# An attention-then-expert-layer kernel: the first chain rebuilt, v block 0 turned on TensorE, the sums of w_out moved later, the last products reordered and their stores spread over three engines

## The chip, the cores and the metric

The kernel runs on one core of one Trainium2 chip. The metric is device time in microseconds (us) of one execution, read as the median of several. A program on one core has no second die to compare with, so a run counts as fast unless it lies over 1.5% above the fastest of its kernel.

## The reference

```python
def attn(q, k, v, tau):                        # q, k, v: 4 x 6080 x 256
    qn = q / (norm(q, axis=1) + 1e-06); kn = k / (norm(k, axis=1) + 1e-06)
    s = kn.transpose(0, 2, 1) @ qn / tau       # 256 x 256 per batch
    a = softmax(s, -1)
    return v @ a
def moe(x, w_in, w_out):                       # x: 24320 x 256
    h = x @ w_in                               # 256 x 2048
    return gelu_tanh(h) @ w_out                # 2048 x 256
```

The score matrix of a batch needs all rows of q and k of that batch. Only then can a product with v start. That is why the first batch has a long start in which DMA is the busy one: in the first three of the 40 slices of the kernel before, DMA is busy at 9 tenths and PE at 3, 7 and 7.

## The kernel before

Per batch the kernel folds the softmax into W_in (`AW = softmax * W_in`, 256 x 2048), so that a block of 512 rows of v needs two stages: `AW` times v (called `mm1`, output tile `hp`, followed by Gelu into tile `g`), and Gelu's output times w_out (`mm2`). The second stage uses seven products on half-size blocks instead of eight, and for this needs seven combinations of quarters of w_out, `wcomb`. There are 48 blocks, 12 to a batch. q and k of the next batch are loaded, squared and multiplied while the blocks of the present one run.

First, w_out as loaded lies in a buffer of the pool that also holds `g`; that pool has two buffers, so `g` of block 1 takes the buffer that w_out leaves. Its load is issued by SP, behind the transpose of v block 1:

```python
    def load_wout():
        w = gp.tile([128, FC, 256], FP32, tag="g", name="wst")
        WST.append(w)
        nc.sync.dma_start(out=w, in_=moe_w_out.rearrange("(t p) d -> p t d", p=128))
    # ... the order of the program:
        cast_v(1)        # GpSimd: v to bf16 in DRAM
        load_vt(1)       # SP: transpose of what the cast wrote
        load_wout()      # SP
```

Second, two of the combinations are plain casts on GpSimd and five are made on DVE (called its sums below). They stand among the eight steps `p` of block 0, ahead of the loads of q and k of batch 1, which GpSimd issues too:

```python
    def prep_wout(step):
        if step == 0:
            nc.gpsimd.tensor_copy(wc(A11), w_half(0, 0))
            nc.gpsimd.tensor_copy(wc(A12), w_half(0, 1))
            # ... DVE sums of steps 0, 1 and 2 left out
    # ... in the loop over blocks n and steps p:
                if n == 0 and p in (2, 4, 5):
                    prep_wout((2, 4, 5).index(p))
                # ...
                    if p in (2, 5) and blk < ncn:
                        load_one(nxt, blk, p // 5, gate)   # q at p == 2, k at p == 5
```

Third, the last block has its second stage alone, in the order of all others, and one store of four DMAs from SP:

```python
        for bi in range(4):
            nc.sync.dma_start(out=dst[bi], in_=ot[bi * 32 : bi * 32 + 32, ...])
```

## Time and profile before

| | before |
|---|---|
| median | 735.85 us (3 runs, 735.68 to 735.98) |
| profiled span | 735.3 us |
| PE busy | 700.1 us (95%) |
| first product with v | 47.09 us |
| last first-stage product | 721.60 us |
| from there to the end of the span | 13.7 us |

The last three rows cut the run into a start, a middle and a tail. PE is busy almost without a gap in the middle, so a change can win or lose only at the two ends. The lines of the profile are in the prediction below. Two more are from the timeline of the kernel before (start, us, engine, line, operation, tiles; in square brackets the idle time before it and what ended it): when GpSimd issues the first load of batch 1, and when the first Gelu of block 1 starts.

```profile
58.96 0.56 POOL L89 DMA_DIRECT2D t<-in_q_dram  x1
64.22 1.02 ACT L325 ACTIVATE g<-hp 128x1024 bf16<-128x1024 f32 x1 [0.73 <-PE hp L321]
```

The load is issued only after w_out has landed (55.42), and the Gelu waits for nothing but PE.

### The profile page before, as it was taken

The page shows a single profiled execution, that of the slowest core. Times are in us where ns is not written, and L with a number is a line of the kernel's source. Part 1 is how long each engine was busy: PE and PEld are TensorE (multiplying, and loading weights), DVE is VectorE, ACT ScalarE, POOL GpSimd, SP SyncE. Part 2 cuts the span into 40 slices and gives each one's busy share as a digit, 9 for nine tenths or more (in the row PEclk, how much of TensorE's full clock was granted, in tenths as well). Part 3 has the DMA queues.
Part 4 walks back from the last instruction along what each step waited for, and adds up shares of the span by engine and source line. Part 5 has one row for each costly group of instructions (what it writes and reads, how often), then busy time and mean ns, then how long its engine had stood idle before and what let it go on. Part 6 is the DMA issues. An engine that isn't in the chain of part 4 may idle for free.

```text
span 735.3 us, 11988 instructions
## 1 busy us (share of the span) xinstructions
PE 700.1 (95%) x4760; PEld 466.6 (63%) x4760; DVE 500.5 (68%) x882; ACT 483.6 (66%) x592; POOL 72.2 (10%) x133
## 2 busy tenths in 40 slices
PE   3777999999999999999999999999999999999996
PEld 2434666666666666666666666666666666666664
DVE  1339787877766787787685777787686465564654
ACT  3365677677667766776666677677666767676672
POOL 4303111110001110110100111111000000000000
PEclk9998999999999999999999999999999999999999
DMA  9995797885437868884455888688334636455233
GB/s 175 203 229 98 123 142 113 129 129 90 67 58 128 135 115 130 133 138 76 77 86 80 130 136 138 108 138 133 56 58 69 100 58 99 74 92 80 47 53 55
DMA packets 164841, 78.65 MB, mean 107 GB/s; under 512 B 152497, under 2 KB 156337, under 8 KB 164017
## 3 DMA queue, kind: packets, MB, share of 16 engines
q0 software_dynamic: 12192, 38.41, 34.0%
q1 hardware_dynamic: 152592, 39.47, 31.7%
q8 instruction: 37, 0.61, 0.3%
q14 instruction: 20, 0.16, 0.1%
HBM read 78.91 MB, written 37.36 MB: 158 GB/s over the span
## 4 chain that ended last, share of the span: by engine, by line
PE 86%; DMA 6%; DVE 4%; issue 1%; ACT 1%; POOL 0%; SPq 0%; DVEq 0%; POOLq 0%
PE hp L321 42%; PE r L414 22%; PE p L414 11%; PE q L414 5%; PE G L175 5%; DMA t<-in_q_dram 2%; DMA t<-in_k_dram 1%; PE ps L297 1%; DMA wst<-in_moe_w_out_dram 1%; DVE dn L274 1%; DMA vb<-in_v_dram 1%; DVE c L430 1%; DVE aw L304 1%; DVE t L385 0%; ACT th L266 0%
## 5 line engine op out<-in xcount | busy, mean ns | idle before, releaser
L325 ACT ACTIVATE g<-hp 128x1024 bf16<-128x1024 f32 (+1 forms) x384 | 387.9, 1015 | 205.3 <-PE hp L321 202.4
L321 PE MATMUL hp<-vT,aw 128*128 128x512 bf16 (+1 forms) x1536 | 389.9, 379 | 4.7 <-DVE aw L304 4.7
L414 PEld LDWEIGHTS <-wcomb 128*128 128x128 bf16 x2688 | 262.7, 98 | 104.7 <-issue 8.8
L321 PEld LDWEIGHTS <-aw 128*128 128x128 bf16 x1536 | 150.3, 98 | 115.2 <-DVE aw L304 5.2
L414 PE MATMUL r<-t,wcomb 128*128 128x256 bf16 (+1 forms) x1152 | 148.0, 271 | 5.2 <-DVE c L430 5.2
L175 PE MATMUL G<-t 128*128 128x256 bf16 (+1 forms) x384 | 69.9, 284 | 16.3 <-DMA t<-in_k_dram 16.3
L430 DVE TENSOR_TENSOR c<-r,y 128x256 f32<-128x256 f32 (+1 forms) x96 | 40.3, 420 | 52.5 <-PE r L414 48.0
L430 DVE TENSOR_TENSOR c<-q,x 128x256 f32<-128x256 f32 (+1 forms) x48 | 20.2, 420 | 73.1 <-PE q L414 71.3
L398 DVE TENSOR_TENSOR t<-t,g 128x1024 bf16<-128x1024 bf16 (+1 forms) x96 | 65.0, 677 | 0.0
L397 DVE TENSOR_TENSOR t<-g 128x1024 bf16<-128x1024 bf16 (+1 forms) x96 | 64.9, 676 | 0.0
L396 DVE TENSOR_TENSOR t<-g,t 128x1024 bf16<-128x1024 bf16 (+1 forms) x96 | 63.4, 661 | 0.1
L137 ACT ACTIVATE sq<-t 128x1536 bf16<-128x1536 bf16 (+4 forms) x31 | 46.2, 1491 | 23.0 <-PE ss L188 12.0
L107 POOL DMA_DIRECT2D vb<-in_v_dram x48 | 24.1, 503 | 365.7 <-PE hp L321 365.2
L438 DVE STREAM_TRANSPOSE ot<-c 128x256 f32<-128x256 f32 (+1 forms) x144 | 57.5, 425 | 2.0 <-DVE c L430 0.4
L385 DVE TENSOR_TENSOR t<-g 128x2048 bf16<-128x2048 bf16 (+1 forms) x48 | 57.7, 1203 | 0.0
L175 PEld LDWEIGHTS <-t 128*128 128x128 bf16 (+1 forms) x384 | 38.7, 102 | 29.7 <-issue 12.0
L414 PE MATMUL r<-g,wcomb 128*128 128x256 bf16 (+1 forms) x384 | 49.4, 272 | 0.0
L414 PE MATMUL p<-t,wcomb 128*128 128x256 bf16 (+1 forms) x384 | 49.3, 271 | 0.0
L414 PE MATMUL q<-g,wcomb 128*128 128x256 bf16 (+1 forms) x384 | 49.3, 271 | 0.0
L414 PE MATMUL p<-g,wcomb 128*128 128x256 bf16 (+1 forms) x384 | 49.3, 271 | 0.0
L138 DVE TENSOR_TENSOR sq<-t 128x1536 bf16<-128x1536 bf16 (+4 forms) x31 | 29.8, 962 | 26.4 <-DMA t<-in_k_dram 26.0
L438 DVE STREAM_TRANSPOSE ot<-r 128x256 f32<-128x256 f32 (+1 forms) x48 | 21.4, 445 | 31.0 <-PE r L414 31.0
(74 smaller groups left out, 293.8 us busy)
## 6 DMA issues: line engine op xcount, KB each, us to landing
out_dram<-ot SPq DMA_DIRECT2D x176, 128.0 KB, 2.9
vb<-in_v_dram POOLq DMA_DIRECT2D x44, 256.0 KB, 5.1
t<-in_q_dram POOLq DMA_DIRECT2D x21, 384.0 KB, 4.9
t<-in_k_dram POOLq DMA_DIRECT2D x21, 384.0 KB, 4.4
t<-in_q_dram POOLq DMA_DIRECT2D x5, 512.0 KB, 13.0
t<-in_k_dram POOLq DMA_DIRECT2D x5, 512.0 KB, 14.9
wst<-in_moe_w_out_dram SPq DMA_DIRECT2D x1, 2048.0 KB, 10.9
out_dram<-ot SPq DMA_DIRECT2D x16, 112.0 KB, 2.7
```

Source lines behind the costliest of these rows:

```text
L137: nc.scalar.activation(sq[:, 0:n, 0:256], qt[:, 0:n, :], AF.Square)
L138: nc.vector.tensor_mul(sq[:, 0:n, 256:512], kt[:, 0:n, :], kt[:, 0:n, :])
L175: nc.tensor.matmul(G[b][:, jc, :], lhsT=qt[:np_, r, jc * 128 : jc * 128 + 128], rhs=kt[:np_, r, :], start=first and jc == 0, stop=last and ...
L321: mm = nc.tensor.matmul(hp[:, u, :cols], lhsT=AW[b][:, cc, fc * 128 : fc * 128 + 128], rhs=vt_tiles[n][:, cc, :cols], start=cc == 0, stop= ...
L325: nc.scalar.activation(GS[n][:, 2 * p : 2 * p + 2, :cols], hp[:, :, :cols], AF.Gelu_apprx_tanh)
L385: nc.vector.tensor_sub(t1[:, :, :hc], quarter(n, 0, 1), quarter(n, 0, 0))
L396: nc.vector.tensor_sub(v[2], b22, v[1])
L397: nc.vector.tensor_sub(v[3], b22, quarter(n, 0, 1, f0, f1))
L398: nc.vector.tensor_sub(v[4], v[2], quarter(n, 1, 0, f0, f1))
L414: nc.tensor.matmul(ACCS[n, acc][:, :hc], lhsT=wcomb[:, w, fc, :], rhs=x, start=first and fc == 0, stop=fc == 7, skip_group_check=True)
L430: nc.vector.tensor_add(CS[n][:, tj, ci, :hc], ACCS[n, acc][:, :hc], XS[n, name][:, :hc])
L438: nc.vector.transpose(OT[n][:, tj * nb : tj * nb + nb, ci, :], src.rearrange("p (x t) -> p x t", t=32))
```

## The change

The intent is to start block 0 sooner and to end the last block sooner. The last chunk of q and k is smaller, and the rows left over go with the first; the norms of q come out of one-column products; v block 0 is no longer cast and transposed by DMA but loaded behind k and turned on TensorE, and fourteen products that nobody uses (`warm`) stand ahead of the score matrix; W_in's first part goes ahead of v; the sums of w_out move to steps 6 and 7 of block 0; and the last block's products have an order in which no two in a row use one accumulator, with its stores cut in halves and spread over three engines. The core of the diff:

```diff
-        sizes = [8, 8, 8, 8, 8, 4, 3] if b == 0 else [6, 6, 6, 6, 6, 6, 6, 5]
+        sizes = [7, 8, 8, 8, 8, 6, 2] if b == 0 else [6, 6, 6, 6, 6, 6, 6, 5]
 ...
-        cast_v(0)
-        load_vt(0)
 ...
         for fs in range(4):
             nc.gpsimd.dma_start(out=win_bf[...], in_=wi[...])
+            if fs == 0:
+                nc.gpsimd.dma_start(out=v0, in_=v[0, 0:BLK, :].rearrange("(s p) c -> p s c", p=128))
         cast_v(1)
         load_vt(1)
         load_wout()
         cast_v(2)
+        warm(14)
         scores(0)
-        row_sums(0)
-        aw_part(0, 0, 0, "dve", "r")
-        aw_part(0, 0, 1, "act", "q")
+        first_vt()
+        first_aw()
 ...
-                if n == 0 and p in (2, 4, 5):
-                    prep_wout((2, 4, 5).index(p))
+                if n == 0 and p in (6, 7):
+                    prep_wout(p - 6)
 ...
+    def mm2_last(n):
+        # ... products 1, 5, 6, 2, 7, 3 with their adds and transposes
+        store_half(n, 1, (nc.sync, nc.gpsimd, nc.sync, nc.gpsimd))
+        product(n, 4, "r", False)
+        turn(n, 1, 0, ACCS[n, "r"][:, :hc])
+        store_half(n, 0, (nc.scalar, nc.sync, nc.scalar, nc.sync))
```

More of the change, by code (lines that the diff above doesn't have):

```diff
@@ L74, in chunks_of, with with_rest @@
         return res
+    def with_rest(b, c):
+        return REM > 0 and c == (0 if b == 0 else len(chunks_of(b)) - 1)
     qk_tiles = {}
@@ L85, in load_one @@
         r0, n = chunks_of(b)[c]
-        last = r0 + n == R
         t = qkp.tile([128, 8, 256], BF16, tag="qk"[which])
@@ L91, in load_one @@
             in_=src[b, 0 : R * 128, :].rearrange("(p r) c -> p r c", r=R)[:, r0 : r0 + n, :]), gate)
-        if last and REM:
+        if with_rest(b, c):
             after(nc.gpsimd.dma_start(out=t[:REM, n, :], in_=src[b, R * 128 : N, :]), gate)
@@ L118, in load_vt @@
         vt_tiles[n] = vT
-    G, SS, ACC, SQ = {}, {}, {}, {}
+    G, SS, ACC, SQ, SQR = {}, {}, {}, {}, {}
     def rows_of(b, c):
@@ L125, in rows_of @@
         rows = [(r, 128) for r in range(n)]
-        if r0 + n == R and REM:
+        if with_rest(b, c):
             rows.append((n, REM))
@@ L132, in squares @@
         r0, n = chunks_of(b)[c]
-        last = r0 + n == R
+        rest = with_rest(b, c)
         sq = sqp.tile([128, 8, 512], BF16, tag="sq")
-        if last and REM:
+        if rest:
             nc.vector.memset(sq[REM:, n, :], 0.0)
-        nc.scalar.activation(sq[:, 0:n, 0:256], qt[:, 0:n, :], AF.Square)
+        if n <= 2:
+            nc.vector.tensor_mul(sq[:, 0:n, 0:256], qt[:, 0:n, :], qt[:, 0:n, :])
+        else:
+            nc.scalar.activation(sq[:, 0:n, 0:256], qt[:, 0:n, :], AF.Square)
         nc.vector.tensor_mul(sq[:, 0:n, 256:512], kt[:, 0:n, :], kt[:, 0:n, :])
-        if last and REM:
+        if rest:
             nc.scalar.activation(sq[:REM, n, 0:256], qt[:REM, n, :], AF.Square)
@@ L142, in squares, with fold_rows @@
         SQ[b, c] = sq
+    def fold_rows(b, c):
+        n = len(rows_of(b, c))
+        if n == 8:
+            a1 = addp.tile([128, 4, 512], BF16, tag="a1")
+            nc.vector.tensor_add(a1, SQ[b, c][:, 0:4, :], SQ[b, c][:, 4:8, :])
+            SQ[b, c] = a1
+            n = 4
+        SQR[b, c] = n
     def sum_rows(b, c):
@@ L179, in gram_row, with ss_rows @@
                 start=first and jc == 0, stop=last and jc == 1)
-    def ss_row(b, c, i):
-        if (b, c, i) == (b, 0, 0):
-            SS[b] = pM.tile([128, 512], FP32, tag="q", name=f"ss{b}")
-        rows = rows_of(b, c)
-        r, np_ = rows[i]
-        first = c == 0 and i == 0
-        last = c == len(chunks_of(b)) - 1 and i == len(rows) - 1
-        nc.tensor.matmul(SS[b], lhsT=ones_bf[:np_, :], rhs=SQ[b, c][:np_, r, :],
-                         start=first, stop=last)
-    def ss_acc(b):
-        nc.tensor.matmul(SS[b], lhsT=ones_f, rhs=ACC[b], start=False, stop=False)
+    def ss_rows(c, which):
+        last = c == len(chunks_of(0)) - 1
+        if c == 0:
+            SS[which] = pM.tile([128, 2] if which == 0 else [128, 256], FP32,
+                                tag="qp"[which], name=f"ss0{which}")
+        sq = SQ[0, c]
+        n = SQR[0, c]
+        for r in range(n):
+            if which == 0:
+                for jc in range(2):
+                    nc.tensor.matmul(SS[0][:, jc : jc + 1],
+                                     lhsT=sq[:, r, jc * 128 : jc * 128 + 128],
+                                     rhs=ones_bf[:, 0:1],
+                                     start=c == 0 and r == 0 and jc == 0,
+                                     stop=last and r == n - 1 and jc == 1)
+            else:
+                nc.tensor.matmul(SS[1], lhsT=ones_bf, rhs=sq[:, r, 256:512],
+                                 start=c == 0 and r == 0, stop=last and r == n - 1)
     def ss_cols(b):
@@ L201, with q_factor @@
     ET, RS = {}, {}
+    def q_factor():
+        lnq = smx.tile([128, 2], FP32, tag="lnq")
+        nc.scalar.activation(lnq, SS[0], AF.Ln, bias=eps)
+        rq = smx.tile([128, 2], FP32, tag="rq")
+        nc.scalar.activation(rq, lnq, AF.Exp, scale=-0.5, bias=log_it)
+        RQ.append(rq)
+    RQ = []
     def scores(b):
-        ss = SS[b]
         lnk = smx.tile([128, 256], FP32, tag="lnk")
-        nc.scalar.activation(lnk, ss[:, 256:512], AF.Ln, bias=eps)
-        qq = smx.tile([128, 2], FP32, tag="qq")
-        for jc in range(2):
-            junk = smx.tile([128, 128], FP32, tag="junk")
-            nc.vector.scalar_tensor_tensor(
-                junk, ss[:, jc * 128 : jc * 128 + 128], 1.0, ident,
-                op0=ALU.mult, op1=ALU.mult, accum_out=qq[:, jc : jc + 1])
+        nc.scalar.activation(lnk, SS[1], AF.Ln, bias=eps)
         rk = smx.tile([128, 256], FP32, tag="rk")
         nc.scalar.activation(rk, lnk, AF.Exp, scale=-0.5)
-        lnq = smx.tile([128, 2], FP32, tag="lnq")
-        nc.scalar.activation(lnq, qq, AF.Ln, bias=eps)
-        rq = smx.tile([128, 2], FP32, tag="rq")
-        nc.scalar.activation(rq, lnq, AF.Exp, scale=-0.5, bias=log_it)
         S = smx.tile([128, 2, 256], FP32, tag="S")
@@ L224, in scores, with first_vt, first_aw, warm @@
         for jc in range(2):
-            nc.scalar.activation(eT[:, jc, :], S[:, jc, :], AF.Exp, scale=rq[:, jc : jc + 1])
+            nc.scalar.activation(eT[:, jc, :], S[:, jc, :], AF.Exp, scale=RQ[0][:, jc : jc + 1])
         ET[b] = eT
+    def first_vt():
+        ps = pM.tile([128, 2, BLK], BF16, tag="r", name="vt_ps")
+        for s in range(BLK // 128):
+            for cc in range(2):
+                nc.tensor.transpose(ps[:, cc, s * 128 : s * 128 + 128],
+                                    v0[:, s, cc * 128 : cc * 128 + 128], ident_bf)
+        vT = vts.tile([128, 2, BLK], BF16, tag="vT", name="vT_first")
+        nc.vector.tensor_copy(vT[:, 0, :], ps[:, 0, :])
+        nc.scalar.activation(vT[:, 1, :], ps[:, 1, :], AF.Copy)
+        vt_tiles[0] = vT
+    def first_aw():
+        b = 0
+        AW[b] = awp.tile([128, 2, D], BF16, tag="aw", name=f"aw{b}")
+        ps = [pM.tile([128, 512], FP32, tag="qp"[ic], name=f"aw_ps{ic}") for ic in range(2)]
+        sums = pM.tile([128, 2], FP32, tag="a", name="sums0")
+        rs = smx.tile([128, 2], FP32, tag="rs")
+        e = lambda jc, ic: ET[b][:, jc, ic * 128 : ic * 128 + 128]
+        for jc in range(2):
+            for ic in range(2):
+                nc.tensor.matmul(ps[ic], lhsT=e(jc, ic), rhs=win_bf[:, jc, 0:512],
+                                 start=jc == 0, stop=jc == 1)
+        for ic in range(2):
+            for jc in range(2):
+                nc.tensor.matmul(sums[:, ic : ic + 1], lhsT=e(jc, ic), rhs=ones_bf[:, 0:1],
+                                 start=jc == 0, stop=jc == 1)
+        nc.vector.reciprocal(rs, sums)
+        RS[b] = rs
+        for f in range(2):
+            for ic in range(2):
+                nc.vector.tensor_scalar_mul(AW[b][:, ic, f * 256 : f * 256 + 256],
+                                            ps[ic][:, f * 256 : f * 256 + 256], rs[:, ic : ic + 1])
+    def warm(n):
+        w = pH.tile([128, 2, 512], FP32, tag="h", name="warm")
+        for i in range(n):
+            nc.tensor.matmul(w[:, 0, 0:256], lhsT=ones_bf, rhs=zeros_bf, start=True, stop=True)
     NRM, TH = {}, {}
@@ L279, in row_sums @@
     def row_sums(b):
-        ps = pM.tile([128, 2], FP32, tag="p" if b == 0 else "q")
+        ps = pM.tile([128, 2], FP32, tag="q")
         for ic in range(2):
@@ L360, in prep_wout @@
         if step == 0:
+            t = sqp.tile([128, 2, 32, 32], FP32, tag="sq", name="wf")
+            WF.append(t)
             nc.gpsimd.tensor_copy(wc(A11), w_half(0, 0))
             nc.gpsimd.tensor_copy(wc(A12), w_half(0, 1))
-            t = sqp.tile([128, 2, 32, 32], FP32, tag="sq", name="wf")
-            WF.append(t)
             nc.vector.tensor_add(t[:, 0], w_half(1, 0), w_half(1, 1))
             nc.vector.tensor_copy(wc(S1), t[:, 0])
+            nc.vector.tensor_sub(t[:, 1], t[:, 0], w_half(0, 0))
         if step == 1:
             t = WF[0]
-            nc.vector.tensor_sub(t[:, 1], t[:, 0], w_half(0, 0))
             nc.vector.tensor_copy(wc(S2), t[:, 1])
             nc.vector.tensor_sub(wc(S4), w_half(0, 1), t[:, 1])
-        if step == 2:
             nc.vector.tensor_sub(wc(S3), w_half(0, 0), w_half(1, 0))
@@ L470, in mm2, with store_half @@
             turn(n, 1, 0, ACCS[n, "r"][:, :hc])
+    def mm2_last(n):
+        hc = cols_of(n) // 2
+        product(n, 1, "r", True)
+        keep(n, "r", "x1")
+        product(n, 5, "p", True)
+        keep(n, "p", "y5")
+        sums_2(n, 4, 8)
+        product(n, 6, "r", False)
+        keep(n, "r", "y53")
+        product(n, 2, "q", True)
+        add_out(n, "q", "x1", 0, 0)
+        turn(n, 0, 0, CS[n][:, 0, 0, :hc])
+        product(n, 7, "r", False)
+        add_out(n, "r", "y5", 1, 1)
+        turn(n, 1, 1, CS[n][:, 1, 1, :hc])
+        product(n, 3, "p", False)
+        add_out(n, "p", "y53", 0, 1)
+        turn(n, 0, 1, CS[n][:, 1, 0, :hc])
+        store_half(n, 1, (nc.sync, nc.gpsimd, nc.sync, nc.gpsimd))
+        product(n, 4, "r", False)
+        turn(n, 1, 0, ACCS[n, "r"][:, :hc])
+        store_half(n, 0, (nc.scalar, nc.sync, nc.scalar, nc.sync))
+    def store_half(n, tj, engines):
+        b, blk = divmod(n, NB)
+        hc = cols_of(n) // 2
+        r0 = b * N + blk * BLK + tj * hc
+        x0 = tj * (hc // 32)
+        dst = out[r0 : r0 + hc, :].rearrange("(x t) (b c) -> b t x c", t=32, b=4)
+        for bi in range(4):
+            engines[bi].dma_start(
+                out=dst[bi],
+                in_=OT[n][bi * 32 : bi * 32 + 32, x0 : x0 + hc // 32].rearrange("p x h c -> p x (h c)"))
     def store(n):
@@ L492 @@
         nc.vector.memset(ones_bf, 1.0)
+        zeros_bf = const.tile([128, 256], BF16)
+        nc.vector.memset(zeros_bf, 0.0)
         ones_f = const.tile([128, 128], FP32)
@@ L500 @@
         nc.vector.memset(log_it, math.log(inv_tau))
+        ident_bf = const.tile([128, 128], BF16)
+        nc.vector.tensor_copy(ident_bf, ident)
         nc.scalar.preload_act_table_set("natural_log_exp_and_others")
         win_bf = const.tile([128, 2, D], BF16)
+        v0 = const.tile([128, BLK // 128, C], BF16)
         wcomb = const.tile([128, 7, 8, 128], BF16)
         nch = len(chunks_of(0))
-        ACCD = nch - 3
         for c in range(nch):
@@ L510 @@
             squares(0, c)
-            if c == ACCD:
-                sum_rows(0, c)
             for i in range(len(rows_of(0, c))):
                 gram_row(0, c, i)
-            if 1 <= c <= ACCD:
-                for i in range(len(rows_of(0, c - 1))):
-                    ss_row(0, c - 1, i)
+            fold_rows(0, c)
             if c == nch - 1:
-                ss_acc(0)
-                for d in (nch - 2, nch - 1):
-                    for i in range(len(rows_of(0, d))):
-                        ss_row(0, d, i)
+                ss_rows(c - 1, 0)
+                ss_rows(c - 1, 1)
+                ss_rows(c, 0)
+                q_factor()
+                ss_rows(c, 1)
+            elif c >= 1:
+                ss_rows(c - 1, 0)
+                ss_rows(c - 1, 1)
         wi = moe_w_in.rearrange("(c p) d -> p c d", p=128)
@@ L530 @@
         cast_v(2)
+        warm(14)
         scores(0)
-        row_sums(0)
-        aw_part(0, 0, 0, "dve", "r")
-        aw_part(0, 0, 1, "act", "q")
+        first_vt()
+        first_aw()
         nc.scalar.preload_act_table(AF.Gelu_apprx_tanh)
         aw_part(0, 1, 0, "dve", "a")
-        aw_part(0, 1, 1, "dve", "p")
+        aw_part(0, 1, 1, "dve", "r")
         NN = B * NB
-        for n in range(NN + 1):
+        for n in range(NN):
             b, blk = divmod(n, NB)
@@ L545 @@
                     keeps(n - 1, p)
-                if n < NN:
-                    if p == 0 and n + 2 < NN:
-                        load_vt(n + 2)
-                    gate = mm1(n, p)
-                    if p == 0 and n + 3 < NN:
-                        cast_v(n + 3, gate)
+                if p == 0 and n + 2 < NN:
+                    load_vt(n + 2)
+                gate = mm1(n, p)
+                if p == 0 and n + 3 < NN:
+                    cast_v(n + 3, gate)
                 if n == 0 and p in (1, 3):
                     fs = 2 + p // 2
-                    aw_part(0, fs, 0, "dve", "r")
-                    aw_part(0, fs, 1, "act", "q")
-                if n == 0 and p in (2, 4, 5):
-                    prep_wout((2, 4, 5).index(p))
+                    aw_part(0, fs, 0, "dve", "q")
+                    aw_part(0, fs, 1, "act", "p")
+                if n == 0 and p in (6, 7):
+                    prep_wout(p - 6)
                 if n >= 1:
@@ L563 @@
                         store(n - 1)
-                if n < NN:
-                    if p == 5:
-                        sums_1(n)
-                    if p == 7:
-                        sums_2(n, 0, 4)
-                if n < NN and nxt < B:
+                if p == 5:
+                    sums_1(n)
+                if p == 7:
+                    sums_2(n, 0, 4)
+                if nxt < B:
                     ncn = len(chunks_of(nxt))
@@ L596 @@
                         aw_part(nxt, p // 2, p % 2, "act" if p % 2 else "dve")
+        mm2_last(NN - 1)
 _INS = ['q', 'k', 'v', 'tau', 'moe_w_in', 'moe_w_out']
```

## The prediction

> **What bounds the kernel now.** I read the page first (engine shares, the 40 slices, the chain that ended last), then the chain in order of time at both ends of the span, then the timeline of the first 90 us and the last 30 us, then busy time and DMA in stretches of 2 us.
>
> From the page:
>
> ```profile
> span 735.3 us, 11988 instructions
> PE 700.1 (95%) x4760; PEld 466.6 (63%) x4760; DVE 500.5 (68%) x882; ACT 483.6 (66%) x592; POOL 72.2 (10%) x133
> PE   3777999999999999999999999999999999999996
> DMA  9995797885437868884455888688334636455233
> PE 86%; DMA 6%; DVE 4%; issue 1%; ACT 1%; POOL 0%; SPq 0%; DVEq 0%; POOLq 0%
> ```
>
> TensorE is the bound from the fifth slice to the last but one. The chain over the first 110 us runs without a gap on PE from 58.83 us, and the one over the last 100 us runs on PE until 726.4. Nothing in the change touches the blocks in between. What can be won lies in the first 64 us, where DMA is the busy row, and in the last 13 us. The start of the chain, with columns start, length, what:
>
> ```profile
> 18.11 17.47 DMA t<-in_q_dram
> 35.58 0.28 issue
> 35.86 7.36 DMA vb<-in_v_dram
> 43.21 0.02 issue
> 43.23 1.23 SPq L117
> 44.46 0.05 issue
> 44.52 10.90 DMA wst<-in_moe_w_out_dram
> 55.42 0.02 issue
> 55.45 1.24 DVE wf L365
> 56.68 0.02 issue
> 56.71 1.41 DVE wcomb L366
> 58.11 0.67 DVE aw L304
> 58.79 0.04 issue
> 58.83 5.30 PE hp L321 x12
> ```
>
> The reader is to see that the chain does not go through the score matrix of the first batch (its first product with v starts at 47.09) but past it: v block 1 is cast, SP waits for that cast, only then issues the w_out load, and everything after hangs on w_out at 55.42. [...] the sums of w_out stand ahead of the second half of A*W_in, and PE waits 4.7 us for it. The granted clock shows what this idling costs besides (columns: PE, PEld, DVE, ACT, POOL busy, PEclk, DMA share, GB/s):
>
> ```profile
> 54.00:56.00 2.00, 0.16 (x1) 0.00 (x0) 0.56 (x1) 1.28 (x2) 0.52 (x1) 1.00 1.06 129
> 60.00:62.00 2.00, 2.00 (x6) 0.76 (x5) 1.97 (x4) 1.02 (x1) 0.06 (x1) 0.50 0.93 110
> ```
>
> At the end, from the timeline:
>
> ```profile
> 726.90 0.93 PE L414 MATMUL r<-t,wcomb 128*128 128x224 bf16 x8 [0.55 <-DVE c L430]
> 728.31 0.93 PE L414 MATMUL r<-t,wcomb 128*128 128x224 bf16 x8 [0.48 <-DVE c L430]
> 729.27 0.42 DVE L438 STREAM_TRANSPOSE ot<-r 128x224 f32<-128x224 f32 x1 [0.41 <-PE r L414]
> ```
>
> Two products in a row on the same accumulator each wait for DVE to read it; after 729.7 four stores and their completion take 5.6 us.
>
> [...] PE idles from about 54.2 to 58.83, the clock is 0.50 until about 64, and eight 512-column products take 0.43 us apart instead of 0.22. [...] Here the four last stores take SP about 0.5 us each to issue (the last of 12 issues ends at 731.66).
>
> **The change part by part.**
>
> Loads. Before, the cast of v block 0 (0.26 MB written) and its DMA transpose (another 0.26 MB) run inside the q/k stream; the 2 us stretches show a steady 210 to 215 GB/s written there. Without them the last k chunk lands (0.52 MB / 213 GB/s =) 2.5 us sooner: 36.7 becomes about 34.2.
>
> From the last k chunk to the first product with v: 36.7 to 47.09 = 10.4 us before (8 rows of 512 columns summed on PE, 1.99 us; the diagonal read-out; Ln to eT 2.8; row sums, then A*W_in). After, worked out from the same rows: products of two rows and the sums of chunk 5 and 6, by columns for q (a 1-column product takes about 0.08) and 256 columns for k, about 2.9; Ln 0.47, Exp 0.42, S 0.42, two Exp 0.91 and handovers, 2.4; A*W_in second half and sums 0.8, reciprocal 0.2, two half-width scalings 0.85 with handovers, 2.1. Sum 7.4, so the first product starts at about 41.7 rather than 47.1. Turning v on TensorE (8 small transposes) and its two PSUM copies lie beside the Ln/Exp steps if v has landed by about 38, which two 0.25 MB pieces behind k (2.5 us) allow. That is 5.4 us of head start for block 0, and the sums of w_out no longer stand before A*W_in on DVE, so block 0 runs its eight steps in about 10 us (ACT: 8 x 1.02 plus 2 x 0.69) and ends near 52. PE alone would then be about 12 us ahead.
>
> But w_out sets the resume. The buffer of w_out is that of g for block 1, so in the order of the changed program the first Gelu of block 1 waits for the DVE and Pool sums of w_out; PE can run only two steps ahead (two hp buffers). So what counts is when w_out lands. The v cast that SP waits for stands behind q, k, W_in and now v: 0.26 MB less than before, so 1.2 us earlier, 42.0; SP takes 1.3 for the transpose, w_out is issued at 43.3 instead of 44.52. Its flight of 10.9 us is the disputed term. Before, q and k of batch 1 were held behind the Pool casts of w_out and issued at 58.96 and 59.52. Now the Pool casts come after them, so these two (0.39 MB each) are issued at about 45.5 and 49 and share the DMA engines with w_out: up to 0.79/213 = 3.7 us. Against that, the cast of v block 3 moves forward into the idle stretch at 43 to 44.5, -1.2. I take half to all of the difference: flight about 12.2, landing at 55.5, no earlier than before.
>
> The sums: 1.24 + 1.41 + 1.39 + 0.69 + 1.22 + 1.22 + 0.68, overlapped 7.6 us as before, but without the scaling of A*W_in in between. Done at 63.1. Then on ACT Gelu 1.02, squares 1.48, keep 0.39, Gelu 1.02: the fourth pair of block 1's first products can start at 67.1. Before, it started at 68.60. Start gain 1.5 us. From there PE is the bound as before.
>
> End. Seven products at 0.77 from 722.35 without a wait: 727.8, then the last transpose at about 728.4 (DVE has an add and two transposes right before) against 729.69: 1.3 us. SP has four half-size issues beginning at 728.0, the last starts at 729.5 instead of 731.2; the GpSimd pair (about 4 us from issue to landing in the page's small loads) begins at 728.0 too and lands about 732.5 to 733. I count 1.4 us for the whole tail.
>
> Middle: nothing. Sum: 735.85 - 1.5 - 1.4 = 732.9.
>
> **The rivals.** (a) The load of w_out is not slowed by q and k of batch 1, and comes earlier with its issue: landing 53.8 to 54, start gain 3.2, total 731.2. For it: before, the DMA rate was only 115 to 280 GB/s in 44.5 to 47 and zero at 53.0 to 53.5, so there is slack. (b) The full 3.7 us goes onto w_out, landing at 57 to 58: start gain 0 to -1, total 734.5 to 735.5; the new wait (Gelu of block 1 for the sums) takes the place of the one removed. [...] (c) The head start carries through, PE saved as if w_out did not matter: 12 + 1.4 = 13 us, 722.5. Against it stands the shared buffer and an issue that cannot come before 42. (d) PE stays at half clock after the resume: [...]
>
> **Range and chances.** The landing of w_out between 53.8 and 57.8 moves the start gain between 3.2 and -0.8; the tail between 0.8 and 1.8; the arrival of k by half a microsecond. Together 729.6 to 735.8. A 2% gain needs 721.1 or less, beyond even rival (c); a 2% loss would need trouble in the blocks between, which are unchanged.
>
> **What would show it.** Right: the last k chunk lands at about 34, the first product with v starts at 41 to 42.5, w_out is issued near 43.3 and lands at 54 to 57, PE has a gap of several us before the first Gelu of block 1, and that Gelu follows the last w_out sum; the last store is issued about 1.5 us sooner after the last first-stage product. Wrong: if block 0's first product is not 4 us or more ahead, the rebuilt chain failed (v late, [...]); if w_out lands before 53 or Gelu of block 1 does not wait for the sums, the gain is larger; if steady blocks change length, something I did not see moved.

Some passages are cut from the text; each cut is marked. None of them is a term of the sum, which still comes to 735.85 - 1.5 - 1.4 = 732.9. One ground of rival (b) is gone, and the ground and the size of rival (d); neither was in the sum.

## The result, and the profile after

| | before | changed | predicted |
|---|---|---|---|
| median, us (4 runs each) | 735.91 | 745.53 | 732.9 |
| range of the runs, us | 735.68 to 737.93 | 744.44 to 746.05 | 729.6 to 735.8 |
| profiled span, us | 735.3 | 744.2 | |
| first product with v, us | 47.09 | 41.79 | 41.7 |
| w_out issued, us | 44.52 | 46.44 | 43.3 |
| w_out landed, us | 55.42 | 59.00 | 55.5 |
| last first-stage product, us | 721.60 | 725.09 | 1.5 sooner |
| from there to the end, us | 13.7 | 19.1 | 1.4 less |

The ratio of changed to before is 1.0123, with a 95% interval of 1.0101 to 1.0144. It is the mean time of one kernel's fast runs over that of the other's of the same rounds, so not quite the ratio of the medians. At a threshold of 2% this is the same time, but the interval leaves out 1: the change costs some 9 us. The last two rows say where: 725.09 - 721.60 = 3.5 us ahead of the tail and 19.1 - 13.7 = 5.4 us at the tail, together the 8.9 us between the spans. The middle adds nothing: the first Gelu of a block is 3.46 us late at block 2 and 3.49 us late at the last block, so the 3.5 us are lost before block 2.

The page of the changed kernel: its span, and the busy tenths of PE and DMA in 40 slices.

```profile
span 744.2 us, 12121 instructions
PE   3776999999999999999999999999999999999993
DMA  9994688776438868874655887786364465563312
```

Against the page before, the fourth slice of PE (55.8 to 74.4 us) has fallen from 7 to 6, and the last one from 6 to 3. So PE stalls a little longer at the start, and stands idle for most of the last 18 us.

**The start.** The chain that ended last, in the changed kernel (start, length, what; `vb` is v in bf16 in DRAM, `wst` is w_out as loaded, `wf` and `wcomb` are its sums, SPq is SP issuing a DMA):

```profile
33.72 9.33 DMA vb<-in_v_dram
...
43.06 3.31 SPq L120
...
46.44 12.56 DMA wst<-in_moe_w_out_dram
...
59.02 1.24 DVE wf L428
...
66.66 0.62 DVE wcomb L436
...
67.44 1.03 ACT g L388
```

It has the same links as before: the cast of v block 1, SP's transpose, the load of w_out, the sums. But SP took 3.31 us at the transpose instead of 1.23, and w_out flew 12.56 us instead of 10.90. The timeline of the changed kernel has the other side of it:

```profile
41.79 1.89 PE L384 MATMUL hp<-vT_first,aw 128*128 128x512 bf16 x8
45.96 0.54 POOL L92 DMA_DIRECT2D t<-in_q_dram  x1 [2.36 <-ACT aw L365]
67.44 1.02 ACT L388 ACTIVATE g<-hp 128x1024 bf16<-128x1024 f32 x1 [15.32 <-DVE wcomb L436]
```

Block 0 is 5.3 us ahead. With it, the load of q of batch 1 is issued at 45.96 (that of k follows at 49.16), 13 us sooner than before and inside the flight of w_out. The first Gelu of block 1 then stands 15.32 us for the last sum of w_out and starts at 67.44 against 64.22: the 3.2 us of loss are there. PE itself stands for GpSimd's first cast of w_out, by its waits (total, times, longest), and before the products that follow the Gelu for 2.02 us more; in the kernel before its one long wait here was 4.7 us.

```profile
PE r L476 <- POOL wcomb L426: 8.9, 1, 8.9
```

PE takes up the first-stage products again at 68.51, and soon after is at half clock, as the windows view shows (window, length, busy time of PE, PEld, DVE, ACT and GpSimd with instruction counts, granted clock, DMA share, GB/s):

```profile
70.00:72.00 2.00, 2.00 (x10) 1.06 (x8) 2.00 (x4) 2.00 (x4) 0.54 (x1) 0.50 0.42 34
```

**The tail.** First the line of the kernel before that marks the last first-stage product, from its timeline:

```profile
721.60 0.92 PE L321 MATMUL hp<-vT,aw 128*128 128x448 bf16 x4
```

And the timeline of the changed kernel from there:

```profile
725.09 0.92 PE L384 MATMUL hp<-vT,aw 128*128 128x448 bf16 x4
...
731.61 0.37 DVE L500 STREAM_TRANSPOSE ot<-r 128x224 f32<-128x224 f32 x1
...
731.98 1.26 POOL L565 DMA_DIRECT2D out_dram<-ot  x2 [55.56 <-DVE ot L500]
732.02 0.92 ACTq L565 DMA_DIRECT2D out_dram<-ot  x2
```

From the last first-stage product to the start of the last transpose it is 6.5 us, and was 7.7 before (721.60 to 729.27): the new order works. The last transfers end by 735.5. What follows is empty, by the windows view:

```profile
736.00:737.00 1.00, 0.00 (x0) 0.00 (x0) 0.00 (x0) 0.00 (x0) 0.00 (x0) 0.50 0.00 0
```

No engine works and nothing moves, and so it stays until the end at 744.2. What fills this time is a DRAIN, an instruction of the closing line of the program; the trace has it at the end of each engine, with at most 1.01 us on the four others in the changed kernel, and does not count it as busy. Here are GpSimd's closing DRAIN instructions (count; shortest, median and longest in ns; starts of the first and last), of the kernel before:

```profile
L627 POOLq DRAIN  x3: 45/102/10547, 672.4 to 735.0; - x3
```

and of the changed kernel:

```profile
L727 POOLq DRAIN  x3: 46/102/10990, 732.5 to 744.0; - x3
```

In both one of the three takes over 10 us, the first one by the trace. In the kernel before GpSimd issued its last load at 672, so its drain was over at 683 (672.4 plus its 10.5), long before PE was done. The changed kernel has GpSimd issue two of the last stores, which puts the same 11 us behind 732.5.

### The profile page after: what moved, and what is told of

It is laid out like the page before. It is cut to its first block, busy times and chain, and to the rows that moved or that the text cites. A ratio compares the mean times of both kernels' runs of the same rounds, so it can differ in the third digit from the quotient of the medians.

```text
span 744.2 us, 12121 instructions
## 1 busy us (share of the span) xinstructions
PE 698.7 (94%) x4824; PEld 469.6 (63%) x4824; DVE 505.4 (68%) x887; ACT 483.1 (65%) x591; POOL 73.7 (10%) x135
## 4 chain that ended last, share of the span: by engine, by line
PE 84%; DMA 7%; DVE 5%; ACT 1%; issue 1%; POOL 0%; SPq 0%; POOLq 0%; DVEq 0%; ACTq 0%
PE hp L384 40%; PE r L476 21%; PE p L476 10%; PE q L476 5%; PE G L191 4%; DMA t<-in_k_dram 4%; DMA wst<-in_moe_w_out_dram 2%; PE ps L360 1%; DVE dn L337 1%; DMA vb<-in_v_dram 1%; DVE c L492 1%; DVE aw L367 1%; ACT g L388 0%; DVE t L447 0%; SPq L120 0%
## 5 line engine op out<-in xcount | busy, mean ns | idle before, releaser
L384 PE MATMUL hp<-vT,aw 128*128 128x512 bf16 (+1 forms) x1504 | 381.7, 378 | 2.2 <-ACT g L388 2.2
L191 PE MATMUL G<-t 128*128 128x256 bf16 (+1 forms) x384 | 71.4, 289 | 16.4 <-DMA t<-in_k_dram 16.4
L143 ACT ACTIVATE sq<-t 128x1536 bf16<-128x1536 bf16 (+3 forms) x30 | 45.6, 1520 | 20.0 <-DMA t<-in_q_dram 17.6
L485 ACT ACTIVATE y<-p 128x256 f32<-128x256 f32 (+1 forms) x95 | 36.4, 383 | 0.6 <-ACT x L485 0.4
```

Source lines behind the costliest of these rows:

```text
L143: nc.scalar.activation(sq[:, 0:n, 0:256], qt[:, 0:n, :], AF.Square)
L191: nc.tensor.matmul(G[b][:, jc, :], lhsT=qt[:np_, r, jc * 128 : jc * 128 + 128], rhs=kt[:np_, r, :], start=first and jc == 0, stop=last and ...
L384: mm = nc.tensor.matmul(hp[:, u, :cols], lhsT=AW[b][:, cc, fc * 128 : fc * 128 + 128], rhs=vt_tiles[n][:, cc, :cols], start=cc == 0, stop= ...
L485: nc.scalar.activation(x[:, :hc], ACCS[n, acc][:, :hc], AF.Copy)
```

## The experiments

There are two theories. For the tail: (T) GpSimd's closing drain starts when GpSimd is done with its last instruction and the program can't end before it. The rival is that the stores themselves or the new order of products are slow. For the start: (S) the loads of q and k of batch 1, now issued inside w_out's flight, hold it up. The rivals are that the new way of v costs something, that the sums in their new place do, and that w_out is late because of where it is issued. Ratios below are to the kernel before of the same chip and call, whose medians there were 736.66, 737.69, 737.24 and 737.20.

**t1: the tail without GpSimd.** The changed kernel with one line altered:

```diff
-        store_half(n, 1, (nc.sync, nc.gpsimd, nc.sync, nc.gpsimd))
+        store_half(n, 1, (nc.sync, nc.scalar, nc.sync, nc.scalar))
```

> The two stores that the changed kernel issues from GpSimd at the very end go to the scalar queue instead; all else is the changed kernel. Theory A (the end of the program waits for GpSimd's own closing drain, 11.0 us in the changed kernel from 732.5 to 743.5; in the kernel before the same drain took 10.5 us but began at 672.9 and was hidden): the idle 7 us at the end go, 738 to 739 us. Theory B (the scalar queue's first use, or the split stores themselves, cost the 7 us): stays at 744 to 746 us.

Measured: 738.87 us, ratio 1.0044 (1.0012 to 1.0077). The last first-stage product is at 724.54 and the span ends at 736.8, so the tail takes 12.3 us instead of 19.1. GpSimd's long drain began at 675.4. The stores from the other engines cost nothing of the kind, and what is left of the loss lies at the start, where w_out's line on the chain reads:

```profile
44.31 14.14 DMA wst<-in_moe_w_out_dram
```

**t2: the old tail on the changed start.** The loop runs to `NN + 1` again with its guards, and `mm2_last` is gone:

```diff
-        for n in range(NN):
+        for n in range(NN + 1):
 ...
-        mm2_last(NN - 1)
```

> The changed kernel with the end of the kernel before (last block in the loop, one store of four pieces from SP). It leaves the start of the change alone. Theory: the start loses 3.5 us (the last first-stage product starts 3.5 us later in the changed kernel's trace), so 739 to 740 us. Rival: the loss is all in the tail, so 735 to 736 us.

Measured: 739.45 us, ratio 1.0044 (1.0022 to 1.0066), tail 13.0 us. So the whole of the tail's loss is GpSimd's part. The times of t1 and t2 can't tell the new order with its stores from the old; in the traces t1's tail is 0.7 us shorter than t2's and 1.4 us shorter than that of the kernel before.

**t3: GpSimd in the tail of the kernel before.** One of the four last stores:

```diff
-            nc.sync.dma_start(
+            (nc.gpsimd if n == NN - 1 and bi == 0 else nc.sync).dma_start(
```

> The kernel before with one change: one of the four stores of the last block is issued from GpSimd. Theory A (GpSimd's closing drain starts after its last DMA and takes about 10.5 us): slower by about 6 to 7 us, 741 to 743 us, with the drain seen from about 730.5 to 741. Theory B (it is not GpSimd): within 1 us of the kernel before.

Measured: 743.70 us, ratio 1.0099 (1.0082 to 1.0116), some 7 us slower from one store and just over the expected 741 to 743; in its trace the tail is 20.0 us (722.62 to 742.6) instead of 13.7. Its drain:

```profile
L627 POOLq DRAIN  x3: 46/93/10823, 731.0 to 742.3; - x3
```

**d1: no DMA, only a late GpSimd instruction.** The kernel before with a copy of 128 x 32 values, whose result nobody uses, behind the last transpose:

```diff
+        if n == NN - 1:
+            late = smx.tile([128, 32], FP32, tag="junk", name="late")
+            nc.gpsimd.tensor_copy(late, ot[:, 0, 1, :])
```

> The kernel before with one small GpSimd copy that waits for the very last transpose, and no late GpSimd DMA. If the closing drain takes its 10.5 us from GpSimd's last instruction of whatever kind, this ends near 742 us with a drain of about 10.5 us from about 730.5. If the 10.5 us belong to the DMA [...], the drain is short after the copy, and the time stays within 1 us of the kernel before.

Measured: 741.46 us, ratio 1.0063 (1.0044 to 1.0082). The copy in the timeline of this run:

```profile
727.76 0.21 POOL L480 COPY late<-ot 128x32 f32<-128x32 f32 x1 [56.83 <-DVE ot L438]
```

and its drain lines:

```profile
L630 POOLq DRAIN  x3: 45/93/10285, 727.7 to 738.5; - x3
```

The long drain begins with a copy of 0.21 us and lasts 10.3 us, and the span ends at 738.8, behind the drain. The tail is 19.2 us (719.60 to 738.8) instead of 13.7. It isn't the store as such, then: a last copy on GpSimd does it as well.

**d2: GpSimd stores that are not last.** t1 with two stores of the third-last block issued by GpSimd, at 712.49:

```diff
-            nc.sync.dma_start(
+            (nc.gpsimd if n == NN - 3 and bi % 2 else nc.sync).dma_start(
```

> The changed kernel without GpSimd stores in the last block, but with two of the four stores of the third last block issued from GpSimd (at about 713, 23 us before the end). If only the time left after GpSimd's last DMA matters, the drain (about 11 us, from 714 to 725) is hidden and the time is that of the run without GpSimd stores, ratio about 1.004, within 1 us. If stores from GpSimd cost as such, it is 2 us slower or more.

Measured: 740.24 us, ratio 1.0037 (1.0019 to 1.0056), against 1.0044 for t1: no cost. Its drain:

```profile
L727 POOLq DRAIN  x3: 46/93/11085, 713.0 to 736.0; - x3
```

The long one began at 713.0 and ended about 724, under the work of PE. With t1, t2, t3, d1 and d2 the tail is settled: T holds and the rivals don't.

**s1: GpSimd's casts of w_out ahead of the loads.** t1 with the two casts back where they hold the loads of batch 1 behind them; the DVE sums stay at steps 6 and 7:

```diff
         if step == 0:
-            nc.gpsimd.tensor_copy(wc(A11), w_half(0, 0))
-            nc.gpsimd.tensor_copy(wc(A12), w_half(0, 1))
 ...
+                if n == 0 and p == 2:
+                    nc.gpsimd.tensor_copy(wc(A11), w_half(0, 0))
+                    nc.gpsimd.tensor_copy(wc(A12), w_half(0, 1))
                 if n == 0 and p in (6, 7):
```

> The changed kernel without the GpSimd stores, and with GpSimd's two casts of w_out put before the loads of q and k of batch 1 in its order, as in the kernel before, so that those loads do not run beside the w_out load. Theory C (these loads slow w_out's flight from 10.9 to 12.6 us): flight back to about 10 to 11 us, w_out lands at about 57 instead of 59, 1.5 to 2 us faster than the run without the GpSimd stores. Rival D (the late issue of w_out, 46.4, and not its flight, sets it): no difference of over 0.5 us.

Measured: 734.98 us, ratio 0.9986 (0.9966 to 1.0006). The chain of this run has w_out's flight:

```profile
45.30 9.72 DMA wst<-in_moe_w_out_dram
```

and its timeline the load of q and the first Gelu of block 1:

```profile
58.56 0.56 POOL L92 DMA_DIRECT2D t<-in_q_dram  x1
63.46 1.02 ACT L388 ACTIVATE g<-hp 128x1024 bf16<-128x1024 f32 x1 [10.93 <-DVE wcomb L434]
```

The flight falls from t1's 14.14 us to 9.72, the Gelu comes at 63.46, and the last first-stage product at 720.95 against t1's 724.54. This is S at its clearest: 3.6 us from the order of two casts and two loads on GpSimd, more than the 1.5 to 2 that I expected. The ratios of t1 and s1 have intervals that do not meet.

**x1: the same order alone, in the kernel before.** The casts move behind the loads:

```diff
-            nc.gpsimd.tensor_copy(wc(A11), w_half(0, 0))
-            nc.gpsimd.tensor_copy(wc(A12), w_half(0, 1))
 ...
+                if n == 0 and p == 6:
+                    nc.gpsimd.tensor_copy(wc(A11), w_half(0, 0))
+                    nc.gpsimd.tensor_copy(wc(A12), w_half(0, 1))
```

> The kernel before with only the order on GpSimd changed as in the changed kernel: its two casts of w_out come after the loads of q and k of batch 1, so these loads are issued during w_out's flight. Theory: w_out's flight lengthens there too, but less than in the changed kernel, as the first block starts 5 us later and with it the loads (q at about 50.5, k at about 53): w_out lands 1 to 2.5 us later, 1 to 2.5 us slower than the kernel before. Rival: no effect on w_out (under 0.5 us), the long flights of the changed kernel having another cause.

Measured: 736.99 us, ratio 0.9996 (0.9981 to 1.0011). My expectation of a loss missed. The timeline shows why:

```profile
50.99 0.56 POOL L89 DMA_DIRECT2D t<-in_q_dram  x1 [2.36 <-ACT aw L302]
```

The loads are tied to steps of block 0, and block 0 starts at 47 here. q comes at 50.99 and k at 54.20, while w_out, issued at 44.51, lands at 56.02 after 11.51 us. So the loss needs two parts of the change together: the casts out of the way of the loads, and the head start that brings the loads forward by five more microseconds. The kernel before has neither, x1 the first alone, s1 the second alone, t1 both; only t1 is slow.

**s3: v block 0 in the old way.** s1 with the cast and the DMA transpose of v block 0 back, and the turn on TensorE gone:

```diff
+        cast_v(0)
+        load_vt(0)
 ...
-        first_vt()
```

> The version with the casts first (735.0), with v block 0 brought in as in the kernel before (cast to DRAM and DMA transpose inside the q/k stream) instead of turned on TensorE. If v's route matters, k's last chunk lands about 2.5 us later and w_out is issued about 1.2 us later. As w_out sets the resume, the loss should be 0.5 to 1.5 us: 735.5 to 736.5 us; if the first DMA transpose of a program is slow to issue by itself, SP's transpose of block 1 takes 1.2 us again instead of 1.5 to 3.3 and the loss is nil.

Measured: 736.69 us, ratio 0.9984 (0.9964 to 1.0004), the same as s1. w_out flew 11.31 us and landed at 56.36, later than s1's 55.02, and the time does not show it. A cost or gain of the new way of v is not seen in the time, whose interval is some 1.5 us either way (0.0020 of 737.69). It is seen at SP, on the chain of this run:

```profile
43.76 1.23 SPq L120
```

The transpose of v block 1 takes SP 1.23 us, as in the four other traces in which SP transposed block 0 before it and w_out comes behind it (before, t3, d1, x1), and not s1's 2.29. In the seven traces without a transpose of block 0 and with w_out behind, it takes 1.35 to 3.31 us; where it is short, 1.45 in t1 and 1.35 in d2, the issue of w_out behind it takes 1.90 and 1.94 us instead of 0.57. So the new way of v makes SP slower on the way to w_out; how it does so is not shown.

**s4: the DVE sums in their old place.** s1 with

```diff
-                if n == 0 and p in (6, 7):
-                    prep_wout(p - 6)
+                if n == 0 and p in (2, 4, 5):
+                    prep_wout((2, 4, 5).index(p))
```

> The version with the casts first (ratio 0.9986), with DVE's sums of w_out back in their old place, in front of the second half of A*W_in. Theory: as in the kernel before, A*W_in then waits for w_out, the last two steps of block 0 and the first of block 1 come after it at half clock, and the first product with w_out starts about wst landing + 8.5 instead of + 2.2; but the Gelu of block 1 waits in both, so the loss is 1 to 2 us. Rival: nil or a gain, so that part of the change was worth nothing.

Measured: 735.56 us, ratio 0.9981 (0.9964 to 0.9998). I had expected a loss of 1 to 2 us and there is none. The waits view of this run, in which a PE line waits for another engine's line (total, times, longest):

```profile
PE hp L384 <- DVE aw L367: 10.0, 1, 10.0
```

PE now waits 10 us in the middle of block 0 instead of at its end. Where PE waits makes no difference that these runs can tell, because the wait ends with w_out either way, whose flight was 8.95 us here.

**w1: w_out sooner, in the kernel before.** The load of w_out goes ahead of the transpose of v block 1 on SP, held until chunk 5 has been multiplied, to keep it behind the loads of q and k:

```diff
-        nc.sync.dma_start(out=w, in_=moe_w_out.rearrange("(t p) d -> p t d", p=128))
+        after(nc.sync.dma_start(out=w, in_=moe_w_out.rearrange("(t p) d -> p t d", p=128)), LAST[0, 5])
 ...
+        load_wout()
         cast_v(1)
         load_vt(1)
-        load_wout()
```

> The kernel before with one change: the w_out load stands ahead of the transpose of v block 1 in SP's order and waits only for the products of q/k chunk 5 (about 35 us), so that it is issued some 9 us earlier. If w_out's landing alone sets the start (as the chain of before says), it lands at about 46 to 48, DVE no longer holds A*W_in back, the 4.7 us wait of PE goes and so does most of the half-clock stretch: 728 to 730 us. Rival: the cast and transpose of v block 1 are now behind w_out and become the wait; then 731 to 735 us.

Measured: 732.16 us, ratio 0.9930 (0.9914 to 0.9947). w_out was issued at 38.30 and landed at 50.9. PE's wait for the second half of A*W_in fell from 4.7 us to 0.4. That w_out sets the start in the kernel before is shown by this run: an issue 6.2 us sooner, and a landing 4.5 us sooner, gave 5.2 us of time (0.0070 of 737.69). It is less than the 728 to 730 us that I expected, as the flight grew to 12.58 us and w_out landed at 50.9 and not at 46 to 48.

**w3: the same on t1.** The edit of w1, with the loads of batch 1 still in the way.

> The changed kernel without GpSimd stores, and with the w_out load issued early (after the products of chunk 5) instead of behind v block 1's cast. Nothing else differs from the run without the GpSimd stores (738.9). Theory: w_out lands at 46 to 48, the first Gelu of block 1 no longer waits for the sums beyond about 57, and the head start of the rebuilt first chain at last counts: 726 to 729 us. Rival (the transpose of v block 1 becomes the wait, landing at 53 or later): 728 to 731 us.

Measured: 735.80 us, ratio 0.9988 (0.9953 to 1.0023). w_out was issued at 35.68 and flew 19.0 us. The waits view has a new entry:

```profile
PE hp L385 <- DMA vT<-vb: 7.4, 1, 7.4
```

Now v block 1, behind w_out on SP, is what PE waits for. Against t1 (issue at 44.31, flight 14.14) the issue is 8.6 us sooner; 4.9 us of it are eaten by the longer flight, and part of the rest moves into the next wait. Both ranges that I had set down, 726 to 729 and 728 to 731, were missed.

**w2: the edit of w1 on s1,** and with the last store uncut, two DMAs from SP and two from ACT:

```diff
-        store_half(n, 0, (nc.scalar, nc.sync, nc.scalar, nc.sync))
+        store(n, (nc.scalar, nc.sync, nc.scalar, nc.sync))
```

> As the run before it, with GpSimd's casts before the loads of batch 1 as well, and the last block stored whole by four DMAs, two from SP and two from the scalar queue. With w_out landed by 48 the order of the casts matters little (under 0.5 us); the four stores instead of eight save up to 1 us: 725 to 728 us.

Measured: 732.78 us, ratio 0.9936 (0.9919 to 0.9954). w_out landed at 51.97 and not by 48, PE waited at most 4.5 us at one time for Gelu, that is for the shared buffer, and the expected 725 to 728 was missed.

**b1: w_out in buffers of its own.** s1 with w_out in two halves, which take a free buffer of A*W_in and a free one of the squares, so that block 1 need not wait for the buffer:

```diff
-        w = gp.tile([128, FC, 256], FP32, tag="g", name="wst")
+        for f, (pool, tag) in enumerate(((awp, "aw"), (sqp, "sq"))):
+            w = pool.tile([128, 8, 256], FP32, tag=tag, name=f"wst{f}")
```

> The version with the casts first (735.0), with w_out loaded into two buffers of its own (two halves, in a free A*W_in and a free squares buffer) rather than into the buffer of g of block 1, so that the first Gelu of block 1 needn't wait for the sums of w_out. If the shared buffer is a real part of the wait (Gelu started 8.4 us after w_out landed, PE idle 2.9 us just before), PE resumes from the first cast on (w_out + 2.1) without a second stop: 2 to 3.5 us faster, 731.5 to 733. Rival: the sums are needed two products later anyway, so under 1 us.

Measured: 733.50 us, ratio 0.9948 (0.9931 to 0.9964), against 0.9986 for s1 on another chip. The first Gelu of block 1 starts at 52.67, right behind block 0, so the buffer wait was real. The edit is worth about 2.8 us by the ratios, but it also cuts the load in two, and the first half landed at 52.2, 2.8 us ahead of the whole in s1; no run parts the buffer from the halves.

**b2: w2 with the buffers of b1.**

> The version with everything (w_out early, casts first, four last stores; ratio 0.9936 to the kernel before), with w_out in its own buffers as well. There PE stood 4.5 us before the Gelu of block 1 although w_out had landed at 52.0. Theory: most of that goes, 3 to 4 us faster, 728 to 730 us; rival: DVE's sums of w_out (8 us) are needed by the third product anyway, 731 to 733 us.

Measured: 730.43 us, just over the expected 728 to 730, ratio 0.9915 (0.9897 to 0.9932), span 728.0. The first half of w_out landed at 47.9, the second at about 52.

**w4: w1 with the new order of the last products,** four stores from SP and ACT, and nothing else of the change:

```diff
+    def mm2_last(n):
+        # ... as in the changed kernel, without the halves
+        store(n, (nc.scalar, nc.sync, nc.scalar, nc.sync))
```

> The kernel before with w_out early (ratio 0.993) and the reordered last products of the change, stored by four DMAs from SP and the scalar queue and none from GpSimd. The reorder saved 1.4 us in the traces and the shared issue of the stores up to 1 us: 1.5 to 2.5 us faster than the run with w_out early alone, ratio about 0.990.

Measured: 730.85 us, ratio 0.9918 (0.9903 to 0.9933). b2 and w4 beat both kernels and can't be told apart. The rebuilt first chain and w_out's own buffers, which b2 has and w4 has not, are together worth nothing that these runs can measure once w_out comes sooner.

## Why the prediction was wrong

The predicted gain was 1.5 us at the start and 1.4 us at the tail. The spans show a loss of 3.5 and 5.4. By its steps:

- **The bound, right.** Only the ends move; the middle has the same length in both kernels.
- **The rebuilt chain, right.** The first product with v starts at 41.79, predicted 41.7.
- **The wait for the shared buffer, right.** The Gelu of block 1 follows the last sum of w_out, after 15.32 us of idling. b1 shows that the buffer is what makes it wait.
- **The issue of w_out, a step that failed: 3.1 us too early.** The prediction had 42.0 for the cast of v block 1, 1.3 us for SP, 43.3 in sum. The cast ended at 43.06, SP took 3.31 us, and the issue came at 46.44. The 1.3 us are those of a kernel in which SP transposes block 0 first. The change takes that transpose away, and s3 shows that SP's time goes back to 1.23 us with it.
- **The loads of batch 1 beside w_out, the other step that failed at the start.** The landing of 55.5 is made of three terms: issue 43.3, flight without the loads 9.7 (10.9 less 1.2), and 2.5 for the loads ("I take half to all of the difference: flight about 12.2, landing at 55.5"). s1 measures the first two, issue 45.30 and flight 9.72, landing 55.02. With the loads w_out landed at 58.45 (t1) and 59.00 (changed), 3.4 to 4.0 us later. So the flight without the loads was right, the loads were undersized by 0.9 to 1.5 us, and the issue in s1 was 2.0 us later than predicted. Rival (b), which put the full 3.7 us on w_out, had the loads right; the issue at 43.3 was wrong for all rivals.
- **Why the flight of 12.56 us looks right and is not a hit.** In the changed kernel's own trace 3.1 of the 3.5 us at the landing are in the issue and 0.4 in the flight. But t1, with the same start, has issue 44.31 and flight 14.14 and lands only 0.55 us sooner, so the near hit of the flight is luck of the draw. The flights with the loads beside w_out from early on were 12.56, 14.14, 14.78 and 13.88 us (changed, t1, t2, d2), with the loads held back 9.72, 11.31, 8.95, 10.90, 12.21 and 9.09 us (s1, s3, s4, before, t3, d1).
- **What the late landing did.** The predicted start gain of 1.5 us was mis-sized by 5.0: 3.5 from the landing, 0.7 from sums that took 8.3 us instead of 7.6 (59.02 to 67.28), and 0.8 left over. The half clock from 70 to 72 is what rival (d) named. It fits the 0.8: on the chain the fourth pair of block 1's first products takes 1.71 us at half clock, and 0.86 in the kernel before. No run took it away alone.
- **The head start, worth nothing that these runs can tell.** With the loads out of the way (s1) the last first-stage product comes at 720.95, 0.65 us before that of the kernel before. But with the start of the kernel before it stands at 719.60, 721.60 and 722.62 in three traces (d1, before, t3), and the ratio of s1, new tail included, is 0.9986 (0.9966 to 1.0006). The 5.3 us of lead at block 0 are lost because w_out and not the score matrix sets the start, as the prediction said.
- **The range, not the sum of its terms.** A start gain between 3.2 and -0.8, a tail gain between 0.8 and 1.8 and half a microsecond for k give 730.35 to 736.35, not 729.6 to 735.8.
- **The last products with their stores, right.** 1.4 us by the traces of before and t1 (13.7 and 12.3), 1.2 of them in the order of the products (7.7 and 6.5).
- **The tail's end, the step that failed most.** The prediction said that "the GpSimd pair" of stores "lands about 732.5 to 733", and counted nothing behind that landing on GpSimd. It counted the flight of a DMA and not what the engine does after its last instruction. The drain of 10.99 us behind 732.5 made the tail 6.8 us longer than t1's. The lines of it were in the trace before, at 672.4, where nothing waited for it. Neither the prediction's rivals nor its list of what would make it wrong had it.

So two terms carry the loss: the drain, 6.8 us between the tails of the changed kernel and t1, and the early loads of batch 1, 3.6 us between the last first-stage products of t1 and s1. Their sum is 10.4; against it stand the 1.4 of the new tail and the 0.65 that s1's trace is ahead of that of the kernel before (SP's slower issue is within it), and 10.4 - 2.05 leaves 8.4 of the 8.9 us between the spans. The missing 0.5 us is the difference between the last first-stage products of the changed kernel (725.09) and t1 (724.54), which differ in nothing at the start; w_out landed at 59.00 and 58.45 there, so it is the spread of its landing.

What stays open: how the new way of v block 0 makes SP slower at the transpose of block 1 (s3 shows only that it does) and why its time varies from 1.35 to 3.31 us, and what GpSimd does in its 10.3 to 11.1 us of drain. All sizes within the start are from one trace a run, and traces of one start lie up to 3 us apart.

## What to carry to other kernels

Look, for each engine, at when its last instruction runs, and at what its closing instructions take, before you give an idle engine the last piece of work: two late stores on GpSimd cost 6.8 us here. When a chain is shortened, follow what its sooner end triggers: loads that hang on steps of the pipeline come forward too (by 13 us here), and may land on the transfer that bounds the start (3.6 us here). And find the transfer that the start waits for last before you rebuild what comes ahead of it: moving one load up the queue was worth 5.2 us here, and the rebuilt chain nothing that the runs can tell.
